# Late passes of an attention and two feed-forward layers: epilogues inside PSUM banks, additions over two banks, split weights kept in DRAM

## The chip, the cores and the metric

The kernel runs on one core of a Trainium2 chip. The metric is the device time of one execution in microseconds. The median of three runs of the kernel before is 1358.69 us (1358.0 to 1359.58).

## What is computed

The inputs q, k, v are 4 batches x 12 heads x 448 positions x 64, in float32; the weights are 768 x 2048 and 2048 x 768, stored as 64-bit floats. The reference, cut to what matters:

```
q_n, k_n = rmsnorm(q, g_q), rmsnorm(k, g_k)
attn = softmax(q_n @ k_n.T / 8)
x = (attn @ v), heads side by side            # 1792 x 768
h = x @ w_in;   x = (s * relu(h)**2 + b) @ w_out       # layer 0
h = x @ w2_in;  out = (h * cos(h)) @ w2_out            # layer 1
```

## The kernel before, in words

**Products in three parts.** Every operand of the two layers is split into a high part, rounded to TensorE's reduced float32, and the rest (`halves` for weights, L380; `split` for activations, L93): ScalarE casts, then VectorE or GpSimd subtracts. `products` (L101) makes three matmuls of a product: high x high, low x high, high x low.

**Stages.** Attention runs over 24 pairs of heads, and between its steps the first pass runs: layer 0 for batches 0 and 1. Then the pools of attention are closed, and three late passes follow (L829): layer 0 for batches 2 and 3, called (0,1), then layer 1 for batches 0 and 1, (1,0), then layer 1 for batches 2 and 3, (1,1). Each late pass has eight chunks of two 128-wide tiles of the inner dimension. A chunk has an input phase (`phase_in`, L698) and an output phase (`phase_out`, L755); the order is in 0, in 1, out 0, in 2, out 1, and so on to out 7.

**Input phase.** It is a two by two block product done with seven products in place of eight. The seven activation operands (11, 2, 3, 1, 21, 4, 22) are prepared once a pass by `prepare_x` (L610), the seven weight operands (11, s2, s3, s1, 12, 22, s4) once a chunk by `prepare_in` (L658): four loads to staging tiles `tf`, four sums on VectorE (L670, L671, L675, L685) and seven splits. The products accumulate in four banks `ph`. VectorE adds them to `u` and `h` in SBUF (`combine`, L720), and `epilogue` (L439) makes g of each of four results, split again. Layer 0: relu (ScalarE, L442), square (GpSimd, L444), affine (VectorE, L446), cast (ScalarE, L461), rest (GpSimd, L462). Layer 1: two range steps on ScalarE (L453, L454), two on VectorE (L456, L457), two more on ScalarE (L458, L459), times h on GpSimd (L460), then the same cast and rest.

**Output phase.** `unit_out_1` (L494, layer 0) has 12 units of six matmuls and 448 columns, `unit_out_2` (L516, layer 1) 14 units of six matmuls and 384 columns, each into one bank of `po_tile` (L488): two of pool `psm` and two of `psb`, in turn. VectorE adds each bank to `acc` in SBUF (L509, L531); in chunk 0 ScalarE copies (L507, L529). `prepare_out` (L689) loads four weight tiles a chunk and splits them.

**Conversion.** The 64 weight tiles of layer 1 have to be converted from 64-bit to 32-bit floats: `convert` (L386) loads raw words, takes two ScalarE and three VectorE instructions (L407 to L409) and stores the result in DRAM. `conversion(3)` asks for one every third step of the late phases, from pass (0,1) on.

**Order.** Each engine works through its instructions in a fixed order that is set when the kernel is built. A list scheduler with a timing model sets it: an instruction can come ahead of its place in the program when its operands and buffers are expected to be there. All DMAs are issued in order on SyncE's queue. Preparation of the next phase is written between the steps of the running one (L844 to L855). `lows` (L606) gives every third split's subtraction to VectorE and the others to GpSimd. `block` (L374) hands out weight tiles: six of pool `wp` and four of `lt`.

## Time and profile before

| | us |
|---|---|
| median of three runs | 1358.69 |
| lowest, highest | 1358.0, 1359.58 |
| the profiled execution | 1357.74 |
| its span, first to last instruction | 1355.9 |

Busy time over the span: TensorE 1237.1 us (91%), VectorE 1091.8 (81%), ScalarE 800.8 (59%), GpSimd 777.4 (57%). The DMAs moved 156.71 MB, 116 GB/s on average. The busy shares are averages over stages with different limits, so each stage is read by itself. In the profile PE is TensorE, DVE VectorE, ACT ScalarE, POOL GpSimd and SP SyncE; L509 is a line of the kernel. A record of an instruction can overlap the next one's start. Matmuls are pipelined: the distance from start to start tells their rate.

### The profile page before, as it was taken

The numbers are of one execution on the slowest core, as the hardware profiler recorded it, in microseconds if no ns is written. First come the engines' busy times: TensorE is split into PE (matmuls) and PEld (weight loads), VectorE is DVE, ScalarE is ACT, GpSimd is POOL, SyncE is SP. The second block draws the span as 40 slices with busy tenths as digits, with TensorE's granted clock in tenths as the row PEclk, the third lists the DMA queues.
The fourth block names the chain that finished last, engine by engine and source line by source line (L and its number), as shares of the span: only waits on it lengthen the run. The fifth ranks groups of instructions, "written<-read, shape, count | busy, mean of one in ns | idle before, by whom it ended". The sixth has DMA issues, their size and how long they took to land. (4 is left out here: it accounts for less than half of the span.)

```text
span 1355.9 us, 19532 instructions
## 1 busy us (share of the span) xinstructions
PE 1237.1 (91%) x6408; PEld 1009.2 (74%) x6408; DVE 1091.8 (81%) x1729; ACT 800.8 (59%) x1813; POOL 777.4 (57%) x785
## 2 busy tenths in 40 slices
PE   5999998989899899968887897899999979999998
PEld 2555666767677676747776786698999969999998
DVE  5888768676766765799899999986887898687875
ACT  4778767655565554446654555457765655866562
POOL 4566548444353431567555556957766787666652
PEclk9999998999999899988989989999999989999999
DMA  4333325443333231676766664251212224222112
GB/s 109 105 92 112 98 69 166 142 125 103 112 115 102 84 107 34 190 240 207 219 193 201 203 202 150 80 178 47 70 53 65 75 74 134 65 59 59 53 48 82
DMA packets 114630, 156.71 MB, mean 116 GB/s; under 512 B 11712, under 2 KB 104544, under 8 KB 114528
## 3 DMA queue, kind: packets, MB, share of 16 engines
q1 hardware_dynamic: 114528, 155.46, 38.0%
q8 instruction: 50, 0.82, 0.3%
q14 instruction: 52, 0.43, 0.1%
HBM read 116.49 MB, written 38.93 MB: 115 GB/s over the span
## 5 line engine op out<-in xcount | busy, mean ns | idle before, releaser
L462 POOL TENSOR_TENSOR gl<-gt,gh 128x448 fp32r<-128x448 f32 x128 | 161.8, 1266 | 68.0 <-ACT gh L461 65.9
L231 ACT ACTIVATE pr<-sc,top 112x448 f32<-112x448 f32 x184 | 116.3, 634 | 69.8 <-DVE top L223 69.5
L523 PE MATMUL po<-wh_o,gh 128*128 128x384 f32 x448 | 151.4, 339 | 6.0 <-DVE acc L531 3.8
L523 PE MATMUL po<-wh_o,gl 128*128 128x384 f32 x448 | 150.0, 335 | 0.0
L523 PE MATMUL po<-wl_o,gh 128*128 128x384 f32 x448 | 149.8, 335 | 0.0
L403 ACT ACTIVATE c<-raw 128x384 f32<-128x384 f32 x128 | 71.1, 556 | 112.0 <-DMA raw<-in_moe_w_in_dram 40.5
L223 DVE TENSOR_REDUCE top<-sc 112x1 f32<-112x448 f32 x192 | 112.9, 616 | 23.2 <-PE sc L211 22.2
L531 DVE TENSOR_TENSOR acc<-po,acc 128x384 f32<-128x384 f32 x196 | 104.6, 550 | 32.3 <-PE po L523 31.8
L249 PEld LDWEIGHTS tp<-ident,pr 112*112 112x112 f32 x768 | 78.5, 134 | 68.6 <-ACT pT L255 13.5
L509 DVE TENSOR_TENSOR acc<-po,acc 128x448 f32<-128x448 f32 x168 | 101.9, 615 | 24.6 <-PE po L500 24.5
L407 DVE SCALAR_TENSOR_TENSOR t<-raw,t 128x384 uint32<-128x384 uint32 x128 | 100.5, 787 | 25.3 <-ACT t L404 24.4
L461 ACT CAST gh<-gt 128x448 fp32r<-128x448 f32 x128 | 72.1, 564 | 79.8 <-DVE gt L446 44.0
L249 PE MATMUL tp<-ident,pr 112*112 112x112 f32 x768 | 102.6, 265 | 12.8 <-ACT pT L255 5.3
L500 PE MATMUL po<-gh,wh_o 128*128 128x448 f32 x192 | 76.0, 397 | 34.6 <-DVE acc L509 31.6
L408 DVE TENSOR_SCALAR c<-c 128x384 f32<-128x384 f32 x128 | 74.7, 586 | 40.4 <-ACT c L403 40.2
L384 POOL TENSOR_TENSOR wl<-t,wh 128x384 fp32r<-128x384 f32 x64 | 68.3, 1075 | 61.8 <-ACT wh L381 61.7
L384 POOL TENSOR_TENSOR wl_o<-tf,wh_o 128x384 fp32r<-128x384 f32 x64 | 75.0, 1178 | 49.1 <-ACT wh_o L381 47.2
L211 PE MATMUL sc<-kT,qT 64*112 64x448 f32 x384 | 99.1, 593 | 0.9 <-DVE kT L202 0.9
L409 DVE SCALAR_TENSOR_TENSOR t<-c,t 128x384 uint32<-128x384 uint32 x128 | 96.7, 757 | 1.1
L523 PEld LDWEIGHTS po<-wh_o,gh 128*128 128x128 f32 x448 | 84.5, 189 | 11.4 <-DVE acc L531 6.4
L460 POOL TENSOR_TENSOR gt<-h_h,gt 128x448 f32<-128x448 f32 x48 | 62.8, 1309 | 50.9 <-ACT gt L459 28.1
L500 PE MATMUL po<-gh,wh 128*128 128x448 f32 x192 | 77.9, 406 | 10.5 <-DVE acc L509 7.4
(156 smaller groups left out, 3764.2 us busy)
## 6 DMA issues: line engine op xcount, KB each, us to landing
tf<-wd SPq DMA_DIRECT2D x192, 192.0 KB, 2.4
raw<-in_moe_w_in_dram SPq DMA_DIRECT2D x64, 384.0 KB, 3.8
wd<-t SPq DMA_DIRECT2D x128, 192.0 KB, 3.4
raw<-in_moe_w_out_dram SPq DMA_DIRECT2D x64, 384.0 KB, 3.3
xr<-yd SPq DMA_DIRECT2D x30, 224.0 KB, 2.7
rawk<-in_k_dram SPq DMA_DIRECT2D x24, 224.0 KB, 3.6
rawv<-in_v_dram SPq DMA_DIRECT2D x24, 224.0 KB, 3.3
yd<-acc SPq DMA_DIRECT2D x24, 224.0 KB, 3.3
```

The source lines that it names most:

```text
L211: mm.append(nc.tensor.matmul(sc[j], st[i]["qT"][half, c * CP:(c + 1) * CP], st[i]["kT"][half, :], start=True, stop=True))
L223: line("DVE", nc.vector.tensor_reduce(tops[j], sc[j], axis=AX.X, op=ALU.max, negate=True))
L231: e = line("ACT", nc.scalar.activation(pr, sc[j], AF.Exp, bias=tops[j], scale=scale[j], accum_out=st[i]["sums"][:, c, j:j + 1]))
L249: mm = [nc.tensor.transpose(tp[:, kc * CP:(kc + 1) * CP], pr[:, kc * CP:(kc + 1) * CP], ident[:CP, :CP]) for kc in range(NCH)]
L384: eng.tensor_tensor(wl, w, wh.bitcast(F32), ALU.subtract)
L407: nc.vector.scalar_tensor_tensor(t, hi, 0x80000000, t, ALU.bitwise_and, ALU.bitwise_or)
L409: nc.vector.scalar_tensor_tensor(t, c, 3, t, ALU.logical_shift_left, ALU.bitwise_or)
L462: nc.gpsimd.tensor_tensor(gl, gt, gh.bitcast(F32), ALU.subtract)
L500: nc.tensor.matmul(po, a, m, start=(f == 0 and n == 0), stop=(f == CF - 1 and n == 2))
L509: nc.vector.tensor_tensor(at, po, at, ALU.add)
L523: nc.tensor.matmul(po, a, m, start=(f == 0 and n == 0), stop=(f == CF - 1 and n == 2))
L531: nc.vector.tensor_tensor(at, po, at, ALU.add)
```

## The change

Eight edits, all in or around the late passes:

- `epilogue_in_bank` takes the place of `epilogue` in the late passes. Layer 0: relu, square, affine and cast are four ScalarE instructions, the first three in place in the bank. Layer 1: cos times h is VectorE's and goes to the bank. The rest `gl` is VectorE's in both. Where a combination is needed, VectorE adds it into a bank (`result`), not into SBUF.
- `po_tile` gives two neighbouring banks in the late passes, in two buffers; a unit fills both (two batches in layer 0, two halves of the model dimension in layer 1), and one instruction adds or copies both. Pool `psm` closes with attention.
- The output weights of layer 0 are stored split (`store`) when the first pass splits them, and loaded split (`recall`) afterwards, in pass (0,1) and at the end of the first pass.
- Pass (1,0) stores its seven split weight operands of each chunk; pass (1,1) loads them and computes none.
- `prepare_in` and `prepare_out` load plain weights straight into the tile of the low part; the four sums and all weight splits of the late passes are GpSimd's.
- `prepare_x` loads further ahead, with nine buffers for six, and splits half of its operands on VectorE and half on GpSimd (`lows`); it moves on two steps for each unit of the last two output phases.
- Conversions are spread by a credit: 6/13 of one per step in pass (0,1) and 2.3/14 in pass (1,0), or on demand.
- Weight tiles: six of `wp` and five of `lt`.

```diff
     def block(key):
-        pool, bufs = (pools["lt"], 4) if "lt" in pools and n % 5 > 2 else (wp, 6)
+        pool, bufs = (pools["lt"], 5) if "lt" in pools and n % 11 > 5 else (wp, 6)
...
+    def store(key, parts):
+        ready[key] = []
+        for n, z in enumerate(parts):
+            d = dram.tile([P, CW], F32, tag=f"r{n}_{key}", name=f"rd{n}_{'_'.join(map(str, key))}")
+            nc.sync.dma_start(d, z.bitcast(F32))
+            ready[key].append(d)
+
+    def recall(key, parts):
+        for z, d in zip(parts, ready[key]):
+            nc.sync.dma_start(z.bitcast(F32), d)
...
     def load_weight(key):
...
+            if (layer, kind, a, e, o) in ready:
+                recall((layer, kind, a, e, o), (hi_part, lo_part))
+                continue
...
             halves(t, hi_part, lo_part, behind=exps[gate + 1] if raws <= 8 and gate + 1 < len(exps) else None)
+            if kind == 1:
+                store((layer, kind, a, e, o), (hi_part, lo_part))
...
+    def epilogue_in_bank(layer, key, h, gh, gl):
         if layer == 0:
...
+            nc.scalar.activation(h, h, AF.Relu)
+            nc.scalar.activation(h, h, AF.Square)
+            nc.scalar.activation(h, h, AF.Identity, scale=sb[:, 0:1], bias=sb[:, 1:2])
         else:
...
-            nc.gpsimd.tensor_tensor(gt, h, gt, ALU.mult)
-        nc.scalar.copy(gh, gt)
-        nc.gpsimd.tensor_tensor(gl, gt, gh.bitcast(F32), ALU.subtract)
+            nc.vector.tensor_tensor(h, h, gt, ALU.mult)
+        nc.scalar.copy(gh, h)
+        nc.vector.tensor_tensor(gl, h, gh.bitcast(F32), ALU.subtract)
...
     def po_tile(key):
...
+        if "psb" in pools:
+            return pools["psb"].tile([P, 2, 512], F32, tag="po", name=f"po_{key}", bufs=2)
+        return pools["psm"].tile([P, 512], F32, tag="mo", name=f"po_{key}", bufs=2)
...
     def lows():
         count["lo"] += 1
-        return nc.vector if count["lo"] % 3 == 0 else nc.gpsimd
+        return nc.vector if count["lo"] % 2 == 0 else nc.gpsimd
...
     def prepare_in(layer, pr, p):
+        names = ("11", "s2", "s3", "s1", "12", "22", "s4")
+        w = late_w["in", layer, pr, p] = {z: block(f"{layer}_{pr}_{p}_{z}") for z in names}
+        if (layer, pr) == (1, 1):
+            for z in names:
+                recall((p, z), w[z])
+                yield
+            return
...
         def operand(what, t):
-            w[what] = block(f"{layer}_{pr}_{p}_{what}")
-            halves(t, *w[what], lows())
+            halves(t, *w[what])
+            if layer == 1:
+                store((p, what), w[what])
...
+        a11, a22, a12 = (fetch(w[z][1].bitcast(F32), *at) for z, at in (("11", (0, 0)), ("22", (1, 1)), ("12", (0, 1))))
+        a21 = fetch(f32("21"), 1, 0)
+        yield
+        s1, s2 = f32("s1"), f32("s2")
+        nc.gpsimd.tensor_tensor(s1, a21, a22, ALU.add)
+        nc.gpsimd.tensor_tensor(s2, s1, a11, ALU.subtract)
...
     def prepare_out(layer, pr, p):
...
+                if layer == 0:
+                    recall((layer, 1, p, eh, f), w[eh][f])
+                else:
+                    low = w[eh][f][1].bitcast(F32)
+                    nc.sync.dma_start(low, fetched(layer, 1, p, eh, f))
+                    halves(low, *w[eh][f])
...
     def phase_in(layer, pr, p):
...
+        def result(f, b, h, u=None, into=None):
+            if u is not None:
+                nc.vector.tensor_tensor(into, h, u, ALU.add)
+                h = into
+            epilogue_in_bank(layer, f"{key}_{f}_{b}", h, *(z[:, b, :] for z in pairs[f]))
...
-        result(1, 1, combine("h", "h11", pd, u3, 3), True)
+        result(1, 1, pd, u3, pb)
...
-        result(1, 0, combine("h", "h10", pc, u2, 3), True)
+        result(1, 0, pc, u2, pc)
...
     def phase_out(layer, pr, p):
         if layer == 0:
             for et in range(NE):
-                for b in range(2):
-                    unit_out_1(late_w["out", 0, pr, p, et // (NE // 2)], p, et, 2 * pr + b)
-                    yield
+                unit_out_1(late_w["out", 0, pr, p, et // (NE // 2)], p, et, (2 * pr, 2 * pr + 1))
+                yield
...
+            for t in range(NT):
+                unit_out_2([late_w["out", 1, pr, p, eh] for eh in range(2)], pr, p, t)
                 yield
...
+    credit = [0.0]
+
     def conversion(rate):
-        while pieces:
-            for _ in range(rate):
-                yield
+        credit[0] += rate
+        while pieces and credit[0] >= 1:
+            credit[0] -= 1
             convert(*pieces.pop(0), late=True)
...
+        if later and p == NCK - 2 and phase is phase_out:
+            soon = [prepare_x(*later[0])]
...
+            if q_ != passes[-1]:
+                conversion(6 / 13 if q_ == passes[0] else 2.3 / 14)
```

## Rows read from the trace of the kernel before

**Rows 1.** Busy time by stretch: us, then PE, PEld, DVE, ACT, POOL (instructions); clock, DMA.
```profile
0.00:561.00 561.00, 519.98 (x2872) 353.14 (x2873) 407.56 (x715) 350.50 (x890) 270.59 (x372) 0.98 0.35 106
561.00:905.00 344.00, 282.24 (x1247) 244.18 (x1246) 324.81 (x489) 176.94 (x373) 208.10 (x166) 0.93 0.63 191
905.00:1050.00 145.00, 142.60 (x753) 134.98 (x752) 114.25 (x167) 94.33 (x195) 101.67 (x84) 1.00 0.22 65
1050.00:1150.00 100.00, 91.94 (x466) 84.62 (x465) 91.80 (x127) 60.67 (x122) 77.10 (x60) 0.97 0.32 96
1150.00:1352.00 202.00, 200.35 (x1077) 192.28 (x1075) 153.36 (x236) 118.36 (x238) 119.98 (x105) 1.00 0.21 59
```

**Rows 2.** TensorE in order of time, 740 to 747 us: start, duration, instruction, idle before.
```profile
740.85 0.37 PE L500 MATMUL po<-gh,wh_o 128*128 128x448 f32 x1
...
742.50 0.37 PE L500 MATMUL po<-gl,wh_o 128*128 128x448 f32 x1
744.66 0.47 PE L718 MATMUL ph_c<-xh,wh 128*128 128x448 f32 x1 [1.79 <-DVE u_u L722]
...
746.69 0.57 PE L718 MATMUL ph_c<-xh,wh 128*128 128x448 f32 x1
```

**Rows 3.** TensorE's waits, 561 to 905 us: total, times, longest.
```profile
PE po L500 <- DVE acc L509: 36.0, 21, 5.3
```

**Rows 4.** VectorE in order of time, 1097 to 1100 us.
```profile
1097.28 0.61 DVE L456 SCALAR_TENSOR_TENSOR gt<-kk,hs 128x448 f32<-128x448 f32 x1
1097.81 0.55 DVE L675 TENSOR_TENSOR tf<-tf,tf 128x384 f32<-128x384 f32 x1
1098.28 1.48 DVE L671 TENSOR_TENSOR tf_s<-tf_s,tf 128x384 f32<-128x384 f32 x1
```

**Rows 5.** Groups, VectorE, 561 to 905 us: count, busy us, mean ns, idle before.
```profile
L509 DVE TENSOR_TENSOR acc<-po,acc 128x448 f32<-128x448 f32 x102 | 61.5, 614 | 4.5 <-PE po L500 4.5
L409 DVE SCALAR_TENSOR_TENSOR t<-c,t 128x384 uint32<-128x384 uint32 x64 | 50.3, 786 | 0.2
L407 DVE SCALAR_TENSOR_TENSOR t<-raw,t 128x384 uint32<-128x384 uint32 x64 | 48.6, 759 | 0.3
L408 DVE TENSOR_SCALAR c<-c 128x384 f32<-128x384 f32 x62 | 39.3, 636 | 7.2 <-ACT c L403 7.1
L446 DVE TENSOR_SCALAR gt<-r,sb 128x448 f32<-128x448 f32 x33 | 25.3, 772 | 0.0
...
L685 DVE TENSOR_TENSOR tf_s<-tf,tf_s 128x384 f32<-128x384 f32 x10 | 9.4, 936 | 0.0
L384 DVE TENSOR_TENSOR wl_o<-tf,wh_o 128x384 fp32r<-128x384 f32 x11 | 8.9, 807 | 0.0
...
L675 DVE TENSOR_TENSOR tf<-tf,tf 128x384 f32<-128x384 f32 x10 | 6.4, 643 | 0.1
...
L384 DVE TENSOR_TENSOR wl_s<-tf,wh_s 128x384 fp32r<-128x384 f32 x3 | 3.2, 1061 | 0.0
```

**Rows 6.** Groups, VectorE, 905 to 1352 us.
```profile
L531 DVE TENSOR_TENSOR acc<-po,acc 128x384 f32<-128x384 f32 x196 | 104.6, 550 | 32.3 <-PE po L523 31.8
...
L456 DVE SCALAR_TENSOR_TENSOR gt<-kk,h_h 128x448 f32<-128x448 f32 x47 | 46.9, 997 | 24.9 <-POOL gl L462 14.2 <-ACT kk L454 10.7
```

**Rows 7.** Groups, ScalarE, 561 to 905 us.
```profile
L442 ACT ACTIVATE h_h<-h_h 128x448 f32<-128x448 f32 x24 | 13.9, 577 | 21.0 <-DVE h_h L722 20.9
```

**Rows 8.** Groups, GpSimd, 561 to 905 us.
```profile
L462 POOL TENSOR_TENSOR gl<-gt,gh 128x448 fp32r<-128x448 f32 x35 | 46.1, 1320 | 23.4 <-ACT gh L461 21.4 <-DMA raw<-in_moe_w_in_dram 2.0
...
L384 POOL TENSOR_TENSOR wl_o<-tf,wh_o 128x384 fp32r<-128x384 f32 x22 | 27.3, 1245 | 38.6 <-ACT wh_o L381 38.6
```

**Rows 9.** Line L411, 561 to 905 us: issues; duration min/median/max ns, first and last start.
```profile
L411 SPq DMA_DIRECT2D wd<-t x64: 319/320/457, 574.4 to 838.4; - x64
```

**Rows 10.** SyncE's waits, 561 to 905 us.
```profile
SPq L411 <- DVE t L409: 52.1, 40, 4.8
```

**Rows 11.** The page's DMA issues: count, KB each, median us to landing.
```profile
tf<-wd SPq DMA_DIRECT2D x192, 192.0 KB, 2.4
```

More of the change, by code (lines that the diff above doesn't have):

```diff
@@ L479, in unit_in @@
         count["g"] += 1
-        epilogue(layer, key, h, gh, gl)
+        epilogue(key, h, gh, gl)
         g[ft, b] = (gh, gl)
@@ L509, in unit_out_1, with unit_out_2 @@
         nc.vector.tensor_tensor(at, po, at, ALU.add)
-        if visits[et, b] < NCK:
+        if visits[et, bs[0]] < NCK:
             return
-        t = dram.tile([P, S], F32, tag=f"y_{b}_{et}", name=f"yd_{b}_{et}")
-        nc.sync.dma_start(t, at)
-        stash[1, b, et] = t
-    def unit_out_2(w, pr, ck, eh, t):
-        key = f"1_{ck}_{eh}_{pr}_{t}"
-        j0 = t * P
-        po = po_tile(key)[:, :EH]
-        for f in range(CF):
-            x = [z[:, j0:j0 + P] for z in g[tile_of(ck, f), "pair", pr]]
-            for n, (a, m) in enumerate(products(x, w[f])):
-                nc.tensor.matmul(po, a, m, start=(f == 0 and n == 0), stop=(f == CF - 1 and n == 2))
+        for k, b in enumerate(bs):
+            t = dram.tile([P, S], F32, tag=f"y_{b}_{et}", name=f"yd_{b}_{et}")
+            nc.sync.dma_start(t, at[:, k, :])
+            stash[1, b, et] = t
+    def unit_out_2(w, pr, ck, t):
+        key = f"1_{ck}_{pr}_{t}"
+        j0 = t * P
+        po = po_tile(key)[:, :, :EH]
+        for eh in range(2):
+            for f in range(CF):
+                x = [z[:, j0:j0 + P] for z in g[tile_of(ck, f), "pair", pr]]
+                for n, (a, m) in enumerate(products(x, w[eh][f])):
+                    nc.tensor.matmul(po[:, eh, :], a, m, start=(f == 0 and n == 0), stop=(f == CF - 1 and n == 2))
         if (1, pr) not in acc:
@@ L734, in phase_in @@
         product(pb, "s2", "2", True)
-        u2 = combine("u", "u2", pb, p1, 3)
+        u2 = combine("u2", pb, p1)
         yield
@@ L772, in body, with fetched @@
         pieces += [(1, 1, p, e, o) for e in range(2) for o in range(CF)]
+    def fetched(*key):
+        while key not in plain:
+            convert(*pieces.pop(0), late=True)
+        return plain[key]
+    credit = [0.0]
     def conversion(rate):
-        while pieces:
-            for _ in range(rate):
-                yield
+        credit[0] += rate
+        while pieces and credit[0] >= 1:
+            credit[0] -= 1
             convert(*pieces.pop(0), late=True)
-    def run(phase, behind):
-        for n, _ in enumerate(phase):
-            for z in behind:
-                next(z, None)
     steps = attention(keep)
@@ L838, in prepared @@
         return (prepare_in if ph[0] is phase_in else prepare_out)(*ph[1:])
-    conv = conversion(3)
     for _ in prepared(phases[0]):
         pass
-    x_next = None
-    for n, ph in enumerate(phases):
+    for n, (phase, *at) in enumerate(phases):
         behind = [prepared(phases[n + 1])] if n + 1 < len(phases) else []
-        if ph[1:] == (0, 1, 0) and ph[0] is phase_in:
-            pass
-        q_ = ph[1:3]
-        if ph[0] is phase_out and ph[3] == NCK - 2 and q_ != passes[-1]:
-            x_next = prepare_x(*passes[passes.index(q_) + 1])
-        extra = [x_next] if x_next is not None and ph[0] is phase_out else []
-        for _ in ph[0](*ph[1:]):
-            for z in behind + extra:
-                next(z, None)
-            next(conv, None)
+        q_, p = tuple(at[:2]), at[2]
+        later = passes[passes.index(q_) + 1:]
+        if later and p == NCK - 2 and phase is phase_out:
+            soon = [prepare_x(*later[0])]
+        for _ in phase(*at):
+            for z in behind:
+                next(z, None)
+            for z in soon:
+                next(z, None)
+                next(z, None)
+            if q_ != passes[-1]:
+                conversion(6 / 13 if q_ == passes[0] else 2.3 / 14)
         for z in behind:
@@ L858, in body @@
                 pass
-        if ph[0] is phase_out and ph[3] == NCK - 1 and x_next is not None:
-            for _ in x_next:
-                pass
-            x_next = None
 _INS = ['q', 'k', 'v', 'g_q', 'g_k', 'moe_w_in', 'moe_w_out', 'moe_s', 'moe_b', 'moe2_w_in', 'moe2_w_out']
```

149 lines of the change are left out of this document (69 added, 80 removed).

## The prediction

> **What bounds the kernel now.** I read the busy time by stretch first, then TensorE's waits in the worst stretch, then VectorE's instructions there. The stretches follow the code: attention and the first pass share 0 to 561 us, the first late pass (layer 0, batches 2 and 3) lies in 561 to 905, and the two passes of layer 1 fill 905 to 1352 [rows 1]. At full clock a matmul of 448 columns starts every 0.206 us (740.85 to 742.50 us, eight steps) [rows 2]. The 1247 matmuls of the first late pass are therefore 1247 x 0.206 = 257 us of work, and the stretch takes 344: 87 us are lost there. After 905 TensorE is busy for 142.6 of 145, 91.9 of 100 and 200.4 of 202 us [rows 1], so at most 12 us are to be had there, 8 of them where the passes of layer 1 meet.
>
> In the first late pass VectorE is busy for 324.8 of 344 us, 94%, against 52% for ScalarE and 60% for GpSimd [rows 1]. TensorE's longest wait there is for VectorE's addition that empties a `po` bank, 36.0 us [rows 3]. Part of the loss is the clock: behind a stall of 1.79 us a matmul's record goes from 0.37 to 0.57 us, the lower of the clock's two levels (1.2 and 2.4 GHz), and the granted clock of the stretch is 0.93 on average against 1.00 after 1150 us [rows 1, 2]. That is given back where the stalls go; I count it within the 87 us. So VectorE bounds this pass, and the late passes of layer 1 are bound by TensorE.
>
> **The change on VectorE, first late pass.** A record overlaps the next: a record of 0.61 us is followed 0.53 us later [rows 4], so 0.08 us are taken from each mean. Removed: the affine step of the epilogue (L446), 33 x (0.772 - 0.08) = 23 us. The four sums of weights per chunk (L670, L671, L675, L685; first and last shown, 40 in all), middle 0.79: 40 x 0.71 = 28 us, now on GpSimd. VectorE's share of weight splits (L384, 33, first and last shown), mean about 0.86: 33 x 0.78 = 26 us, either on GpSimd or replaced by loads. Of the 102 additions at L509, 84 belong to the late pass and become 42 over two banks; they cost 84 x 0.534 = 45 us now [rows 5]. All removed: 122 us.
>
> Added: 42 additions of 896 columns. The trace has none, but 448 columns take 0.614 and 384 take 0.550 us [rows 5, 6], 1.0 ns a column; so 0.614 + 0.448 - 0.08 = 0.98, 41 us together. The bounds are 0.93 (columns alone) and 1.07 (two single ones); I take the value the column price gives. `gl` moves from GpSimd: 32 instructions with one input in a bank and one in SBUF, the operands of L509, at 0.534: 17 us. Half instead of a third of the x splits on VectorE: 6 more at about 1.06 - 0.08, 6 us. All added: 64 us. The five combinations per chunk stay; they only write elsewhere.
>
> So VectorE's work goes from 325 to 325 - 122 + 64 = 267 us. The 64 conversions of layer 1's weights all ran inside this pass, at 0.786 + 0.759 + 0.636 - 0.24 = 1.94 us each [rows 5], although the program asks for fourteen of them later: the order of issue pulls them forward. The change asks for 48 here and 16 in the next pass. If those 16 stay there, 31 us more go, and VectorE has 236. The two bounds, 236 and 267, lie on either side of TensorE's 257. I take the stretch at 278: TensorE's 257 and 21 for its beginning, where x and the first weights are prepared (VectorE's idle time before was 19, most of it unavoidable), and for stalls that remain. That is **-66**. Bounds: 262 (-82) and 300 (-44), the latter being 267, the 19 idle, and 14 of waits for banks.
>
> The other engines have the room. ScalarE gains two instructions for each of 32 results at 0.577 us [rows 7], 37, and loses the 32 casts of the output weights at about the same price, 18: 196 of 278 us. GpSimd loses `gl` (35 x 1.320), the square (32, priced like its other instructions) and the 22 splits of the output weights, and takes 40 sums and 22 splits at 1.245 [rows 8]: 208 - 46 - 40 - 27 + 50 + 27 - 7 (x splits) = 165 us, 59% of 278 against 60% before.
>
> **Two banks per instruction.** The `po` buffers were four banks of which TensorE could be three ahead; they are now two pairs. A pair is filled in 12 x 0.206 = 2.5 us and its addition takes 0.98, so VectorE may come 1.5 us late before TensorE stops; with four single banks it was 3 x 1.24 - 0.53 = 3.2. VectorE's contended instructions last up to 1.48 us [rows 4], so one of them in front is covered, two are not. Nothing where VectorE has slack; part of the 14 us above where it has none.
>
> **Results finished in their bank.** A bank of `ph` is held until ScalarE and VectorE have done the whole epilogue, six instructions and some 4 us, and no longer only up to the combination. What hides this is the output phase in between, 72 x 0.206 = 14.8 us of TensorE. Zero; without that cover it would be 4 us a chunk.
>
> **Layer 1's passes, 905 to 1352.** VectorE loses half of its instructions at L531 and all preparation of weights, and takes cos times h and `gl`; L456 reads a bank [rows 6]. VectorE isn't the bound there: 114 + 92 + 153 = 359 us busy in 447 [rows 1]. The second pass over layer 1 loads its split weights and prepares nothing. I expect some of the 8 us at the meeting of the passes and some new waits for the bank pairs: **-3**, bounds -10 (most of the 12 idle) and +12 (112 pairs at 0.1 us).
>
> **Stores and loads.** Added on SyncE's queue: 64 stores of split output weights during attention, for 32 plain ones; 64 loads for 32 in the first late pass; 112 stores in the next one and 112 loads for 32 in the last. An issue takes 0.32 us and the store of a conversion waited in 40 cases of 64, 52.1 us in all, 1.3 each [rows 9, 10]. Behind a waiting store stand the loads of raw weights, of x and of q, k, v. In attention that is 32 x (0.32 + 1.3) = 52 us more of a queue over 561 us, with work prefetched; the weights' buffers are also held until the store lands. Bounds 0 and +8, taken **+2**. In the late passes it is a rival (below).
>
> The sum: -66 - 3 + 2 = -67. The profiled execution took 1357.74 us (span 1355.9 and 1.84 around it), 0.95 below the median 1358.69. So 1357.74 - 67 + 0.95 = **1292 us**; with its own bounds about 1270 to 1318.
>
> **Rivals.**
> 1. *TensorE never waits.* The 16 conversions stay late and VectorE has 236 us. For it: after 950 us the same loops run with next to no gaps. Against it: at the start of the pass x must be prepared whatever follows. 260 in the stretch, -8 later: 1358.69 - 84 - 8 = 1267.
> 2. *VectorE stays the bound.* All conversions run early again, in the first half of the pass, since the order of issue fills every gap; bank pairs make each late addition a stall. For it: that is how they ran before, and two inputs in SBUF make one instruction 0.55 or 1.48 us long [rows 4]. 298 in the stretch, +12 later, +2: 1358.69 - 46 + 14 = 1327. The Trainium skill, SBUF — State Buffer, section Who interferes with whom, says that a VectorE instruction with two SBUF inputs contends with GpSimd for a port that is locked for a whole instruction. By that rule the sums that go to GpSimd still hold up the conversions, and VectorE gets less back than the instruction counts say; the pairs of rows above agree with it.
> 3. *Slower: the queue starves the weights.* Weights now load straight into the operand's buffer, with no staging buffer in front, so a chunk's preparation can only begin when the chunk before has left its buffers. Its first operand needs the landing, 2.4 [rows 11], three sums and one split on GpSimd, 4 x 1.245 [rows 8]: 7.4 us, inside the 14.8 of the output phase. In layer 1's first pass SyncE has about 27 issues a chunk, 8.6 us, and if each of 14 stores waits 1.3 us as above, 18 more: 27 us of about 29. When loads come over 7.4 us late TensorE waits; from 12 us late in each of 15 chunks of two passes the gain is gone. At 14 late: 15 x 6.6 = 99 us, 1391. Against it: the loads are issued ahead of the chunk's stores.
> 4. *The change doesn't reach the bound*, gain and new waits cancel: within 0.2%.
>
> **How the numbers follow.** Forecast 0.58, first rival 0.14, second 0.20, third 0.06, fourth 0.02. A measurement of this kernel tells about 0.2% from no change. All of the first three are faster: 0.92; same 0.02; slower 0.06. The range takes in the forecast's bounds, rival 1's end and most of rival 2: 1266 to 1330.
>
> **What would show it.** Right: the first late pass in about 280 us, VectorE below 95% in it, waits for `acc` well under 36 us, the clock near 1.00; L509 in pairs at about 1.06 us. Wrong: conversions that all end in the first half of the pass with VectorE full; TensorE waiting for weight splits or for loads in 905 to 1130; attention ending later than 570.

## The result, and where the time went

| | before | after |
|---|---|---|
| median, us | 1358.35 | 1341.74 |
| lowest to highest | 1357.55 to 1359.58 | 1341.06 to 1342.54 |
| span of the profiled execution | 1355.9 | 1339.3 |
| busy: TensorE, VectorE | 1237, 1092 | 1232, 976 |
| busy: ScalarE, GpSimd | 801, 777 | 779, 577 |
| moved by DMAs, MB | 156.7 | 207.8 |

The ratio is 0.9877, with a 95% interval of 0.986 to 0.9894: 1.2% less, clear of noise and the way that was forecast, but by 16.6 us and not by 67. 1341.7 lies above the range of 1266 to 1330.

Three points in the order of TensorE's matmuls tell where it came from: the last input matmul of the first pass, the first matmul of pass (1,0), and the end.

| stretch, us | before | after | moved | predicted |
|---|---|---|---|---|
| attention and first pass, to its last input matmul | 560.4 | 556.7 | -3.7 | +2 |
| from there to the first matmul of pass (1,0) | 299.6 | 286.4 | -13.2 | -66 |
| from there to the end | 495.9 | 496.2 | +0.3 | -3 |

So the miss lies in the first late pass, and almost all of it there. The prediction's own stretches (to 561 and 905 before, to 557 and 892 after, with 2872 and 1247 matmuls against 2868 and 1251) say the same: they moved by -4, -9 and -4 us. Busy time by stretch, after, with the columns of [rows 1]:

```profile
0.00:557.00 557.00, 517.05 (x2868) 350.22 (x2868) 409.97 (x719) 351.54 (x892) 270.61 (x372) 0.99 0.38 118
557.00:892.00 335.00, 280.82 (x1251) 248.65 (x1251) 269.79 (x385) 191.59 (x396) 154.26 (x135) 0.90 0.74 237
557.00:652.00 95.00, 66.54 (x256) 56.87 (x257) 83.22 (x114) 48.99 (x103) 51.86 (x43) 0.77 0.78 253
652.00:850.00 198.00, 181.88 (x841) 162.69 (x841) 161.45 (x243) 127.51 (x264) 78.36 (x70) 0.96 0.71 220
850.00:892.00 42.00, 32.40 (x157) 29.09 (x155) 25.12 (x30) 15.08 (x30) 24.05 (x23) 0.94 0.80 278
892.00:1050.00 158.00, 157.79 (x821) 149.73 (x822) 103.56 (x153) 98.31 (x194) 87.32 (x84) 0.98 0.44 147
1050.00:1100.00 50.00, 42.76 (x224) 40.89 (x223) 44.32 (x61) 31.18 (x63) 31.84 (x26) 0.93 0.47 147
1100.00:1337.00 237.00, 233.08 (x1248) 223.03 (x1246) 148.34 (x225) 105.98 (x206) 32.48 (x32) 1.00 0.43 134
```

The second line answers to 561 to 905 in [rows 1] (1251 matmuls for 1247). VectorE's busy time fell from 324.8 to 269.8 us, as worked out, and its share from 94% to 81%. It no longer fills the stretch, and yet the stretch only went from 344 to 335 us. With 0.206 us a matmul [rows 2], TensorE lost 95 - 256 x 0.206 = 42 us in the first 95, 198 - 841 x 0.206 = 25 in the next 198 and 42 - 157 x 0.206 = 10 in the last 42. All three lie where the DMAs are busy for 71 to 80% of the time, and at the start the granted clock is 0.77. From 892 on hardly anything is lost, as before.

The waits of the stretch 557 to 892 (of SyncE: to 900), TensorE first (total, times, longest). The fifth line is from 850 to 900 us: this wait ends at 892.2, behind the edge, and is nearly all of the last 10 us.

```profile
PE ph_a L763 <- DVE gl L483: 8.1, 3, 6.3
PE po L523 <- DVE acc L532: 7.4, 6, 2.8
PE ph_b L763 <- ACT wh_s L380: 6.4, 1, 6.4
PE ph_c L763 <- DVE u_u L767: 6.4, 3, 5.0
...
PE ph_a L763 <- DVE gl L483: 9.8, 1, 9.8
...
POOL tf_s L710 <- DMA wl<-wd: 118.2, 8, 23.5
...
SPq L396 <- DVE t L406: 38.2, 24, 3.2
SPq L393 <- DVE t L406: 35.7, 18, 4.6
SPq L411 <- DVE t L408: 34.4, 40, 2.8
```

The wait of [rows 3], 36.0 us for `acc`, is down to 7.4. The loss is now in many short waits for weights, activations and additions, and in two longer ones for a bank that the epilogue still holds: 6.3 us at 631.75 and 9.8 at 892.2, each at the second chunk of a pass. What stands out is off TensorE, but neither of the two waits there tells where TensorE's time goes. GpSimd waits 118 us at the first sum of a chunk (L710) for a raw weight to land; it waits 114 in a1 below, which converts nothing, and TensorE loses nothing from 652 to 830 there. SyncE stands for 108 us, a third of the stretch, at the conversions' own transfers, raw loads (L393, L396) and stores (L411), until VectorE has done its part, and the loads of the late pass are queued behind these. Before, the same three waits came to 120.7 us, the stores' 52.1 of [rows 10] and those of the raw loads:

```profile
SPq L397 <- DVE t L407: 36.7, 24, 4.4
SPq L394 <- DVE t L407: 31.9, 24, 5.5
```

So the standing queue is not new. New is that three of a chunk's four raw weights have no staging tile in front.

### The profile page after: what moved, and what is told of

Same layout as the page of the kernel before. It is cut to its first block, busy times and chain, and to the rows that moved or that the text cites. A ratio compares the mean times of both kernels' runs of the same rounds, so it can differ in the third digit from the quotient of the medians.

```text
span 1339.3 us, 19446 instructions
## 1 busy us (share of the span) xinstructions
PE 1231.5 (92%) x6408; PEld 1012.5 (76%) x6408; DVE 976.0 (73%) x1539; ACT 778.6 (58%) x1749; POOL 576.5 (43%) x647
## 4 chain that ended last, share of the span: by engine, by line
PE 52%; DVE 17%; ACT 11%; DMA 10%; issue 6%; POOL 4%; SPq 1%; ACTq 0%; POOLq 0%; DVEq 0%
PE po L548 17%; PE po L523 8%; PE ph_a L763 5%; DMA raw<-in_moe_w_in_dram 5%; PE ph_d L763 4%; PE ph_c L763 4%; DVE t L406 4%; ACT pr L230 3%; PE av L271 3%; PE sc L210 3%; PE ph_b L763 3%; PE ph L494 2%; DMA raw<-in_moe_w_out_dram 2%; PE tp L248 2%; DVE t L408 2%
## 5 line engine op out<-in xcount | busy, mean ns | idle before, releaser
L383 POOL TENSOR_TENSOR wl_o<-wl_o,wh_o 128x384 fp32r<-128x384 f32 x64 | 67.0, 1058 | 230.9 <-ACT wh_o L380 214.4
L556 DVE TENSOR_TENSOR acc<-po,acc 128x768 f32<-128x768 f32 x98 | 93.2, 952 | 53.0 <-PE po L548 52.7
L532 DVE TENSOR_TENSOR acc<-po,acc 128x448 f32<-128x448 f32 (+1 forms) x126 | 96.8, 772 | 35.9 <-PE po L523 35.7
L406 DVE SCALAR_TENSOR_TENSOR t<-raw,t 128x384 uint32<-128x384 uint32 x128 | 102.4, 801 | 26.5 <-ACT t L403 24.1
L407 DVE TENSOR_SCALAR c<-c 128x384 f32<-128x384 f32 x128 | 69.9, 548 | 59.7 <-ACT c L402 59.4
L408 DVE SCALAR_TENSOR_TENSOR t<-c,t 128x384 uint32<-128x384 uint32 x128 | 93.3, 731 | 1.9
L548 PEld LDWEIGHTS po<-wh_o,gl 128*128 128x128 f32 x448 | 84.5, 189 | 1.2
L548 PEld LDWEIGHTS po<-wl_o,gh 128*128 128x128 f32 x448 | 84.4, 189 | 0.3
L710 POOL TENSOR_TENSOR tf_s<-tf,wl 128x384 f32<-128x384 f32 x16 | 17.7, 1104 | 147.0 <-DMA wl<-wd 144.8
L271 PE MATMUL av<-pT,rawv 112*64 112x448 f32 x384 | 79.4, 548 | 0.2 <-DVE pT L252 0.2
```

The lines of the kernel that those rows point to most:

```text
L271: mm.append(nc.tensor.matmul(st[i]["pa"][j * D:(j + 1) * D, :], st[i]["v"][:, j, kc, :], st[i]["pT", j][:, kc, :], start=(kc == 0), stop=( ...
L383: eng.tensor_tensor(wl, w, wh.bitcast(F32), ALU.subtract)
L406: nc.vector.scalar_tensor_tensor(t, hi, 0x80000000, t, ALU.bitwise_and, ALU.bitwise_or)
L408: nc.vector.scalar_tensor_tensor(t, c, 3, t, ALU.logical_shift_left, ALU.bitwise_or)
L532: nc.vector.tensor_tensor(at, po, at, ALU.add)
L548: nc.tensor.matmul(po[:, eh, :], a, m, start=(f == 0 and n == 0), stop=(f == CF - 1 and n == 2))
```

## The experiments

Theory Q: the first late pass is set by SyncE's queue. The 64 conversions hold it, and the chunk's weights, which lost their staging tiles, come late. The expectations of a11, a12, a13 and a15 call its first half theory F (weight loads wait behind the conversions' transfers), against their theory E (the load of transfers and instructions together makes a chunk's preparation longer than the time it has). Rival V, the prediction's own reason: it is VectorE's time. Rival E, another thing than theory E: banks held by the epilogue. Rival P: the pairs of banks. "Lost" is TensorE's time as above, the duration less 0.206 us for each matmul. Each kernel's ratio is to the kernel before, on the same chip; differences between kernels are taken from the medians, and by the ratios they come out up to 4 us otherwise.

### Parts of the change undone

**a3_sbuf_epilogue** combines into SBUF again and runs the epilogue there, so that a bank is free after its combination.

```diff
-                nc.vector.tensor_tensor(into, h, u, ALU.add)
-                h = into
-            epilogue_in_bank(layer, f"{key}_{f}_{b}", h, ...)
+                nc.vector.tensor_tensor(t, h, u, ALU.add)
+            epilogue_in_bank(layer, f"{key}_{f}_{b}", t, ..., h if u is None else None)
```

> The changed kernel with the late epilogues in SBUF again: VectorE's combination, or ScalarE's first step, goes to one of three SBUF tiles and the steps after it work there; the engines of each step stay as changed. A bank is free after the combination. Theory A: VectorE's subtraction has two inputs in SBUF again and gets slower beside GpSimd, so 1342 to 1352. Theory B (held banks): the waits of 6.3 and 9.8 us for a bank at the second chunk of the passes go, 1320 to 1330. Theory C: no change within 5 us.

1341.32 us, ratio 0.9883 [0.9861, 0.9904]: no change. The 8.1 us of waits for `gl` are gone and 11.3 us of waits for `wl` are there for 3.6 (one staging tile fewer, to make room). Since the edit frees the banks and takes a staging tile away, and staging counts (below), it does not settle what the held banks cost.

**a4_single_banks** gives `po` its four single banks back.

```diff
-            return pools["psb"].tile([P, 2, 512], F32, tag="po", name=f"po_{key}", bufs=2)
+            return pools["psb"].tile([P, 512], F32, tag="po", name=f"po_{key}", bufs=4)
...
-        nc.vector.tensor_tensor(at, po, at, ALU.add)
+        for k, po in enumerate(pos):
+            nc.vector.tensor_tensor(at[:, k, :], po, at[:, k, :], ALU.add)
```

> The changed kernel with four single po banks and one addition or copy for each bank, as before. Theory A: VectorE has about 84 more fixed costs in the first late pass and 98 later, 5 to 8 us of its time; 1342 to 1350. Theory B (pairs): TensorE's waits for acc (6.8 us in 652 to 850, 7.2 at 1050 to 1100) go, 1325 to 1335. Theory C: no change within 5 us.

1347.81 us, 0.993 [0.991, 0.9949]: the pairs are worth 6 us. Rival P falls, they help.

**a10_vector_sums** gives VectorE the four sums of a chunk and a third of the weight splits again.

```diff
-            halves(t, *w[what])
+            halves(t, *w[what], lows3())
...
-        nc.gpsimd.tensor_tensor(s1, a21, a22, ALU.add)
+        nc.vector.tensor_tensor(s1, a21, a22, ALU.add)
```

> The changed kernel with the four sums of weights on VectorE again and every third split of weights there, as before. VectorE gets back some 40 us in the first late pass (from 270 to 310 of 335). If VectorE's room is what let the conversions cost less than before: 1350 to 1360. If not: 1338 to 1345.

1341.88 us, 0.988 [0.9865, 0.9895]: no change. The sums and splits that the change moved to GpSimd, 28 and 26 us by the prediction, could have stayed. But VectorE's busy time in 557 to 892 went only from 269.8 to 274.5 us, not to the expected 310, while GpSimd's fell from 154.3 to 90.5: beside a less busy GpSimd the conversions' instructions are shorter. Their first, after and in a10:

```profile
L406 DVE SCALAR_TENSOR_TENSOR t<-raw,t 128x384 uint32<-128x384 uint32 x62 | 48.6, 784 | 2.4 <-ACT t L403 0.5
...
L406 DVE SCALAR_TENSOR_TENSOR t<-raw,t 128x384 uint32<-128x384 uint32 x62 | 39.4, 637 | 2.2 <-ACT t L403 0.5
```

So a10 does not fill VectorE and says little on rival V. It shows that the move itself gave VectorE next to nothing.

### What the conversions cost

**a1_noconv** leaves the 64 late conversions out, their loads and stores too; the later passes read other weights of the same size. **b1_before_noconv** is the same in the kernel before.

```diff
+        if late:
+            plain[layer, kind, a, e, o] = plain[0, 0, a, e, o] if kind == 0 else ready[0, 1, a, e, o][0]
+            return
```

> The changed kernel with the 64 conversions of layer 1's weights left out (no raw loads, no ScalarE, VectorE or store work for them); layer 1 takes layer 0's weights from DRAM instead, so its output is another. Theory A, conversions crowd the start of the first late pass and slow its preparation: 557 to 652 us shrinks from 95 to about 60, the rest of the pass from 198 to about 180, total about 1285 to 1295. Theory B, the bank pairs and the banks held by the epilogue set the waits: 5 to 15 us less than 1341.7, about 1330. Theory C, the loads and stores on the queue are what is late (recalled weights, x): the raw loads are half of the bytes there, so about 1310, with VectorE far below 80% and TensorE still waiting at the start.

> The kernel before with its 64 late conversions left out; layer 1 takes layer 0's weights, so its output is another. If VectorE's total bounds the first late pass of the kernel before (325 us of 344, 124 of them conversions), the pass falls to TensorE's 257 and some 25 us: about -60, 1298, hardly above the changed kernel without conversions (1295), and the rest of the change is worth a few us only. If the other VectorE work removed by the change counts by itself, it stays near 1320.

1294.86 us, 0.9543 [0.9523, 0.9563], and 1295.36, 0.9532 [0.9508, 0.9557]. Without conversions the two kernels take the same time. They cost 63 us before and 47 after, and this difference is all that the change gained. Where nothing is converted, all its parts together come to nothing.

**a2_pinned** keeps each conversion at its place in the program: its raw load waits for the last ScalarE cast written before it, so it can't run ahead. **b2_before_pinned** does that in the kernel before.

```diff
-            convert(*pieces.pop(0), late=True)
+            convert(*pieces.pop(0), marks.get("act"), late=True)
```

> The changed kernel with the conversions kept, but each held behind the ScalarE instruction of the last epilogue (or of the first product's copy) written before it, so that it cannot run ahead of its place. Theory A: the start of the pass loses six or more of its conversions, the middle takes them; 1310 to 1325. Theory B: as the changed kernel within 5 us. Theory C: a few us less, 1335, since the bytes are only spread.

> The kernel before with its conversions held behind the last ScalarE instruction of an epilogue or first copy written before them, as in a2_pinned. If the place of the conversions is most of what costs, it gains as the changed kernel did, 10 to 20 us: 1340 to 1349. If VectorE's total bounds the pass of the kernel before (325 of 344 us), moving conversions back only shifts where it is full: within 5 us of 1358.

1326.07 us, 0.9778 [0.9743, 0.9814]: 16 us. In the kernel before only 4: 1354.78, 0.9975 [0.9964, 0.9986]. This and b1's 1295 are what was expected if VectorE's time bounds the kernel before; transfers move or go in both runs too, so they don't prove it.

**a5_pinned_dma_only** keeps of the pinned conversions the load of the raw words and a store of their bytes, and computes nothing. **a6_pinned_compute_only** keeps the five instructions, on one raw tile loaded once, and no transfers.

> The changed kernel with only the DMAs of the conversions, each raw load waiting for the ScalarE instruction that a2_pinned's conversion was held behind, and the store taken from the raw words; no ScalarE or VectorE work for them, layer 1 takes layer 0's weights, so its output is another. Theory A (VectorE's time and place): 1295 to 1302, as without conversions. Theory C (bytes on the queue): 1315 to 1326, as a2_pinned.

> The changed kernel with only the ScalarE and VectorE instructions of the conversions, pinned as in a2_pinned, all on one raw tile that is loaded once, without the other 63 loads and without the stores; layer 1 takes layer 0's weights, so its output is another. Theory A: 1315 to 1326. Theory C: 1295 to 1302. If both parts cost half, 1310 in both.

1303.98 us, 0.9605 [0.9579, 0.9631], and 1301.28, 0.9579 [0.9557, 0.9601]: alone they cost 9 and 6 us (a6's interval overlaps a1's), together 31. Each of the two theories expected one of them to be the whole cost; neither is. Busy time, 652 to 830 us, of a1, a2, a5 and a6:

```profile
652.00:830.00 178.00, 176.07 (x869) 162.64 (x868) 88.82 (x112) 80.58 (x164) 79.18 (x77) 1.00 0.38 122
...
652.00:830.00 178.00, 170.44 (x822) 152.68 (x820) 148.73 (x215) 112.32 (x235) 73.05 (x66) 1.00 0.67 211
...
652.00:830.00 178.00, 172.22 (x843) 157.29 (x842) 85.40 (x108) 80.19 (x165) 78.67 (x76) 1.00 0.73 232
...
652.00:830.00 178.00, 174.89 (x854) 159.57 (x854) 155.73 (x221) 113.95 (x240) 86.35 (x76) 1.00 0.35 108
```

The last line settles rival V for the pinned kernel. VectorE is fuller there than in a2, 155.7 of 178 us (87%), and TensorE makes 854 matmuls for 822. The third shows that the DMAs' share alone is not it either: 73% busy, and 843 matmuls.

**a9_decoupled** is a2 with all transfers and all instructions, but the instructions work on a fixed tile, so that no raw load and no store waits for VectorE (one staging tile fewer). **a11_no_hold** is a9 with transfers of as many bytes from DRAM to DRAM, which hold no tile and wait for none.

```diff
+            d = dram.tile([P, CW // 2], I64, tag=f"w_{kk}", name=f"wd_{kk}")
+            nc.sync.dma_start(d, raw[:, :CW // 2])
...
+            lo = hi = still.bitcast(U32)
```

> Both halves of the conversions at once, but not joined: the loads and stores of a5_pinned_dma_only, and the ScalarE and VectorE instructions of a6_pinned_compute_only on one fixed tile in SBUF, both pinned; layer 1 takes layer 0's weights, so its output is another. The same bytes and the same engine time as a2_pinned. If load alone counts: 1320 to 1326. If it is the joining (ScalarE and VectorE, which work in order, wait for a raw tile's landing, and the queue waits for VectorE): 1305 to 1312, the sum of the two halves (9 and 6 us over 1295).

> As a9_decoupled (1323), but the DMAs of the conversions are copies from DRAM to DRAM that read and write as many bytes (288 KB each way), wait for nothing and are only ordered behind the last weight load written before them; the ScalarE and VectorE instructions stay on one fixed tile, pinned. Layer 1 takes layer 0's weights, so its output is another. Theory F, waits of conversions at the head of SyncE's queue hold up the weight loads behind them: 1300 to 1308. Theory E, DMA load and engine load together make the preparation of a chunk's weights longer than the time it has: 1316 to 1324.

1323.2 us, 0.9743 [0.9729, 0.9758], and 1310.36, 0.9642 [0.9628, 0.9657]. That a transfer waits for VectorE itself is worth 3 us, within the intervals; a9 came out where load alone was expected to put it. That it holds no tile and waits for none is worth 13 more, and then the two halves cost what they cost alone (1294.9 + 9 + 6 = 1310). But the DMAs are also less busy with these copies (0.48 for 0.68 in 652 to 830), and by a5 up to 9 us could be due to that. So a11, between the ranges of its two theories, points to the standing queue and doesn't prove it.

### Other places and other queues

**a7_pinned_gap** asks for no conversion in the first two chunks' input phases and the last two output phases of a pass, and for more in the next pass; **a8_pinned_even** likewise, with more in the first (7.4 / 13 and 3.6 / 14).

```diff
-            if q_ != passes[-1]:
-                conversion(6 / 13 if q_ == passes[0] else 2.3 / 14)
+            if q_ != passes[-1] and not (phase is phase_in and p < 2) and not (phase is phase_out and p >= NCK - 2):
+                conversion(6 / 13 if q_ == passes[0] else 4.7 / 14)
```

> As a2_pinned, and no conversion is written in the first two input phases and the last two output phases of a pass; what is left over goes to layer 1's first pass at 4.7 per chunk, where VectorE is busy for two thirds. Theory A: the beginning and the ends of the passes come near those without conversions: 15 to 25 us less than a2_pinned's 1326, 1302 to 1310. Theory C: within 5 us of 1326.

> As a7_pinned_gap, with 7.4 conversions a chunk in the middle of the first late pass (44 of 64) and 3.6 a chunk in layer 1's first pass. In a7_pinned_gap the first late pass was as short as without conversions (832.8 against 827.5 us at its end) and 30 us were lost at 1000 to 1100, where the next chunk's weights were converted just before they were needed. If lateness was the cause there, that loss goes and the first pass stays within 8 us: 1305 to 1318. If conversions cost wherever they lie, it stays at 1326 to 1337.

1336.75 us, 0.9846 [0.9827, 0.9864], and 1333.21, 0.9811 [0.9793, 0.9829]: against what I expected a7 is worse than a2, and a8 no better (its interval overlaps a2's). In a7 the last output matmul of the first late pass ends at 832.8, near the 827.5 of a1, but 100 - 357 x 0.206 = 26 us are lost from 1000 to 1100 (1 in a1), where `ph_b` waits 12.6 us for `wh_s`: weights converted just before they are wanted come late.

```profile
1000.00:1100.00 100.00, 77.11 (x357) 70.61 (x356) 74.08 (x114) 52.15 (x107) 39.12 (x35) 0.85 0.55 173
```

In a8 `ph_a` waits 11.0 us for `wl` from 652 to 830, which fits weights that come late as well.

**a12_gpsimd_queue** and **a13_scalar_queue** are a2 with the conversions' transfers issued by GpSimd or by ScalarE.

```diff
-            dma = nc.sync.dma_start(raw, ...)
+            dma = (nc.gpsimd if late else nc.sync).dma_start(raw, ...)
```

> a2_pinned with the raw loads and the stores of the late conversions issued by GpSimd (busy for half of the pass) and not by SyncE. Theory F: the weight loads no longer queue behind them, 1302 to 1315, less what GpSimd's own waits cost. Theory E: 1320 to 1335.

> a2_pinned with the raw loads and the stores of the late conversions issued by ScalarE. Theory F: 1305 to 1318. Theory E: 1320 to 1335. In both, ScalarE waits for VectorE at each store, so it may be worse than with GpSimd.

1335.36 us, 0.9831 [0.9816, 0.9846], 9 worse; 1321.36, 0.9725 [0.9703, 0.9747], 5 better, with intervals that just touch. On GpSimd's queue the conversions' transfers stand in front of splits and sums: they wait 69 us for VectorE (L393 and L396, 557 to 900), and issuing them takes 42 of the 110 us for which GpSimd is busy in 652 to 830 (73 in a2). Both runs came out in theory E's range or at its edge, not in F's. In a13 no conversion is in SyncE's queue, and yet GpSimd's wait for raw weights is nearly that of a2. In 557 to 892, a2 and then a13:

```profile
POOL tf_s L710 <- DMA wl<-wd: 104.3, 8, 19.6
...
POOL tf_s L710 <- DMA wl<-wd: 88.9, 7, 19.2
```

### The staging given back

**a15_staged** is a2 with six staging tiles `tf` for four, all raw weights loaded into them and none into the operand's tile; the x pieces pay with seven buffers for nine. **a16_staged_only** is the changed kernel with this and without the pinning. **a17_staged_noconv** is a1 with it.

```diff
-            return load(temp("xr", f"{layer}_{pr}_{what}_{c}", 9), b, c)
+            return load(temp("xr", f"{layer}_{pr}_{what}_{c}", 7), b, c)
...
-            return pools["lt"].tile([P, CW], F32, tag="tf", ..., bufs=4)
+            return pools["lt"].tile([P, CW], F32, tag="tf", ..., bufs=6)
...
-        a11, a22, a12 = (fetch(w[z][1].bitcast(F32), *at) for z, at in ...)
+        a11, a22, a12 = (fetch(f32(z), *at) for z, at in ...)
```

> a2_pinned with the plain weights of prepare_in loaded to staging tiles again (six tf; seven xr in place of nine), so that the loads and the sums need not wait until the chunk before has left its operand tiles. Theory E: the preparation has its slack back, 1300 to 1312. Theory F: 1320 to 1330.

> The changed kernel with its conversions where the change put them (free to run ahead), and with the two staging rooms that the change took away given back in part: six tiles instead of four for the raw weights' staging, and all three raw quarters of a chunk copied into them rather than read out of the operand tile; the x pieces have seven tiles instead of nine to make room. Theory A (the lost time is chunks' weights that come late because SyncE holds their loads behind the conversions' DMAs, and staging gives them a chunk's head start): the gain is the one that the same edit had on the pinned kernel, some 16 us, so 1322 to 1328, and GpSimd's wait at the 11-sums for a load nearly disappears. Theory B (staging only helps when the conversions are kept at their place, because those that run ahead take the whole queue at the start of the pass): 1336 to 1343, no change by over 0.4%.

> The kernel without the 64 late conversions (the later passes read the split weights of the first pass instead, so that the operand values differ), with the same staging edit. It asks whether staging is worth anything where no conversion stands in SyncE's queue. Theory A (staging only covers for loads held behind the conversions' DMAs): 1292 to 1297, as without staging. Theory C (a chunk's weights come late in any case, and staging shortens the starts of the passes too): 1278 to 1288, and the 25 us that TensorE loses between 550 and 650 fall below 18.

1309.64 us, 0.9628 [0.9608, 0.9648]; 1322.02, 0.9734 [0.9718, 0.9751]; 1283.51, 0.9447 [0.9426, 0.9467]. Staging is worth 16 us beside the pinning, 20 alone, and 11 even where nothing is converted. a15 does all of the work and beats both kernels: 32 us below the changed one, 49 below the one before. Its time lies in theory E's range (1300 to 1312), a17's in that of its theory C: staging helps without any conversion too.

GpSimd's waits at the first sum of a chunk, 557 to 892 us, in a1, a16 and a17:

```profile
POOL tf_s L713 <- DMA wl<-wd: 113.9, 10, 18.3
...
POOL tf_s L710 <- DMA tf<-wd: 7.4, 4, 3.3
...
POOL tf_s L713 <- DMA tf<-wd: 4.0, 4, 1.9
```

And SyncE's in a1 (557 to 900), where no conversion is in the queue:

```profile
SPq L698 <- PE ph_a L766: 46.2, 11, 6.7
SPq L698 <- PE ph_c L766: 36.8, 14, 7.4
```

This is what loading without staging looks like. L698 is the load of a raw weight (L695 in the changed kernel). It goes into an operand's tile, and SyncE stands until TensorE has left that tile: 83 us, and GpSimd's 114 behind them. With staging both are gone, but others take their place (in a17 GpSimd waits 89 us for ScalarE's casts), and from 652 to 830 a1 loses nothing with them. So they are not the cost. Busy time 652 to 830 and 830 to 930 of a17, then 830 to 930 of a1:

```profile
652.00:830.00 178.00, 176.83 (x870) 162.96 (x870) 96.28 (x122) 88.83 (x175) 81.10 (x78) 1.00 0.40 126
830.00:930.00 100.00, 99.75 (x525) 94.65 (x524) 64.95 (x100) 64.76 (x130) 60.81 (x60) 1.00 0.59 197
...
830.00:930.00 100.00, 88.31 (x450) 83.06 (x449) 64.50 (x94) 62.27 (x125) 60.47 (x56) 0.93 0.51 175
```

The 11 us come where the two passes meet (525 matmuls for 450, clock 1.00 for 0.93), and most of them are a single wait of TensorE for a held bank. Its waits for `gl`, a1 from 795 to 860 and a17 from 557 to 892:

```profile
PE ph_a L766 <- DVE gl L486: 10.4, 1, 10.4
...
PE ph_a L766 <- DVE gl L486: 0.6, 1, 0.6
```

In a1 46 of the 63 matmuls of pass (1,0)'s first chunk come behind the last output unit of pass (0,1), at 827.5 us. The second chunk follows at once, and TensorE stands 10.4 us, until 847.25, for a bank that the first chunk's epilogue still holds. In a17 the first chunk's matmuls all lie among the output units, from 796 to 832 us, and nothing is waited for. That staging lets the next pass's weights be expected earlier, so that the order of issue comes out so, is likely and not shown. With conversions it is the same: this wait is 9.8 us after and 7.6 in a2, 1.3 in a15 and gone in a16, and from 830 to 930 a16 makes 505 matmuls for 421 and a15 467 for 430, against 767 for 761 and 829 for 822 from 652 to 830.

At the start of the pass nothing is gained: 557 to 652 loses 95 - 364 x 0.206 = 20 us in a1 and 95 - 359 x 0.206 = 21 in a17, so that half of the expectation was wrong.

## Why the prediction was wrong

- **The term that failed** is the stretch 561 to 905, "I take the stretch at 278: TensorE's 257 and 21 for its beginning". It measured 335. What the prediction works out is the pass without conversions: in a1 557 to 652 loses 20 us and 652 to 830 none. The step took VectorE's busy time for all that conversions cost, and asked only whether its sum falls below TensorE's. It did, and a6 shows that VectorE 87% busy hardly holds TensorE up (854 matmuls from 652 to 830 for a1's 869). But the conversions cost 47 us, 16 of them by running ahead (a2) and 31 at their place (a2 less a1), of which 9 and 6 are seen alone. And weights without staging cost 11 us where nothing is converted (a17) and 16 to 20 where the conversions share the queue (a15, a16); the sum had nothing for that either. The forecast's bounds are also added wrongly: its terms give 1267 to 1335, not 1270 to 1318.
- **The sums of the engines were right.** VectorE 269.8 us (predicted 267, the upper bound with all 64 conversions; 62 were in the stretch), ScalarE 191.6 (196), GpSimd 154 (165), TensorE's 257. The prices were right too:

```profile
L532 DVE TENSOR_TENSOR acc<-po,acc 128x896 f32<-128x896 f32 x42 | 45.4, 1083 | 16.5 <-PE po L523 16.5
L483 DVE TENSOR_TENSOR gl<-ph_b,gh 128x448 fp32r<-128x448 f32 x9 | 5.5, 614 | 1.8 <-ACT gh L482 1.8
...
L556 DVE TENSOR_TENSOR acc<-po,acc 128x768 f32<-128x768 f32 x98 | 93.2, 952 | 53.0 <-PE po L548 52.7
```

  A two-bank addition takes 1083 ns (estimated 1.06), `gl` from a bank 614, as L509's operands in [rows 5]. The wait for `acc` fell as expected, but not through the pairs: with single banks (a4) it is 4.2 us.
- **In-bank epilogue, costed at nothing:** mis-sized. The prediction said that without the cover of an output phase it would cost 4 us a chunk. At the second chunk of passes (0,1) and (1,0) that cover is missing, and TensorE waits 6.3 us (until 631.75) and 9.8 (until 892.2). The second wait is most of what staging gives back in a17. a3 takes both away and gains nothing, but with a staging tile fewer, so the net cost of the hold is open.
- **Attention, +2 (0 to +8):** -3.7, outside its bound. The 32 more stores cost nothing, and something else there got shorter; I made no experiment on it.
- **Layer 1, -3 (-10 to +12):** +0.3, or -4 by the prediction's own stretch. No net cost of the 112 stores and loads is seen.
- **Rival 3** ("the queue starves the weights") had the premise word for word: no staging tile in front, so a chunk's preparation begins when the chunk before has left its buffers. I looked for it at 14 stores a chunk in pass (1,0), where it didn't happen, and wrote "in the late passes it is a rival" with a chance of 0.06, as an all or nothing of 99 us. The loss of staging cost some 20 us (a16), most of it where passes (0,1) and (1,0) meet; TensorE's longest stop there, 9.8 us, is for the held bank and not for weights. [rows 10] also gave the queue's waits too low: 52.1 us are the stores' alone, and the raw loads' 68.6 stand in the same view. Rival and forecast were no alternatives: part of rival 3 belonged into the forecast's sum.
- **Rival 2** (all conversions early, 1327) had the condition and lies nearest the result, but its cause, VectorE as the bound with stalls at the pairs, is not borne out by a4 (pairs help) and a6. What it said of the sums on GpSimd, that VectorE gets less back than their count says, is what a10 shows. Its early conversions do cost: 16 us by a2, 12 in the staged kernel (1322.0 to 1309.6). At the start of the pass they meet the preparation of x and of the first weights. VectorE in order of time there, then at a quiet place:

```profile
597.62 1.16 DVE L407 TENSOR_SCALAR c<-c 128x384 f32<-128x384 f32 x1
598.69 1.35 DVE L406 SCALAR_TENSOR_TENSOR t<-raw,t 128x384 uint32<-128x384 uint32 x1
600.08 1.24 DVE L408 SCALAR_TENSOR_TENSOR t<-c,t 128x384 uint32<-128x384 uint32 x1
...
700.46 0.36 DVE L407 TENSOR_SCALAR c<-c 128x384 f32<-128x384 f32 x1
700.74 0.55 DVE L408 SCALAR_TENSOR_TENSOR t<-c,t 128x384 uint32<-128x384 uint32 x1
701.20 0.55 DVE L406 SCALAR_TENSOR_TENSOR t<-raw,t 128x384 uint32<-128x384 uint32 x1
```

  A conversion takes 3.75 us of VectorE at the start and 1.46 later. GpSimd has an instruction of 1.1 to 1.5 us in nearly every place from 592 to 615 us. From 696 to 704 it has none. The Trainium skill, SBUF — State Buffer, section Who interferes with whom, says that a VectorE instruction with two inputs in SBUF contends with a GpSimd instruction that reads SBUF. The trace agrees for L406 and L408 (0.55 us, and 1.24 to 1.35 beside GpSimd). L407, with one input, is slower too; the section names `tensor_scalar` in a two-port mode, and no run here shows which mode it had.
- **The signs I named** were mostly seen, and the time missed all the same: VectorE below 95% (81%), waits for `acc` well under 36 us (7.4), attention before 570, pairs at 1.06. Only the clock (0.90 for near 1.00) and the duration itself spoke against it.

By steps, the changed kernel comes down so: 1341.7, conversions kept at their place 1326.1, staging back 1309.6, no conversions 1283.5. Some 26 us are left for the conversions themselves, 9 and 6 of it seen alone in a5 and a6. A loss of 15 us or more in 557 to 652 is there in every kernel looked at, with conversions or without (b1: 95 - 386 x 0.206 = 15). Why transfers and instructions cost more together in a9, where neither waits for the other, than alone is not settled: a11 leaves held tiles and the DMAs' load as causes. So theory Q is shown only in its second half, that weights without staging cost time; what the queue's standing is worth stays open, and a9, a12, a13 and a15 speak more for the load of both together.

## What to carry to other kernels

A sum of busy times is a lower bound for each engine, and a stretch that is longer than all the sums is bounded by something that has no busy time. Here the same work was nearly free as transfers alone and as instructions alone, and dear as both; and a change that removed staging buffers cost most at one place, where the next pass's first chunk came late in TensorE's order and a bank was still held. A long wait of an engine off the critical path is no loss by itself: GpSimd's 114 us cost nothing in the middle of a1's pass. Read TensorE's own gaps first, also those that cross the edge of a window, and set a wait against the same wait in the kernel before, all lines of it. And leave the work out that you take for harmless: one run without the conversions said more than all the sums.

## What the hardware showed that I had not expected

- Costs that don't add up: the same 64 conversions cost 9 us as transfers, 6 as instructions and 31 as both, and 15 when the transfers hold no tile (a11, with the DMAs less busy).
- Work moved off VectorE to GpSimd came back as longer VectorE instructions: 40 sums and 23 splits moved back to VectorE in a10 raise its busy time by 4.7 us, since a conversion's three instructions fall from 784, 738 and 575 ns to 637, 586 and 405.
- A one-input instruction of VectorE between SBUF tiles (L407, 384 columns) takes 0.36 us alone and 1.16 beside GpSimd, three times as long; a subtraction with one input in a bank (L483) stayed between 0.606 and 0.625 throughout the pass.
- The clock makes a slow start slower: 557 to 652 us was granted 0.77 after and 0.93 without conversions. A matmul's record was 0.74 us at 631.75, behind a stall of 6.27, against 0.36 at full speed.
- DMAs busy for 73% (232 GB/s) cost the kernel only 9 us in a5, where no transfer waited for VectorE.
